# Attention masks copied ahead of the values' low part, and the buffers of two weights opened at the end of the ordered stretch

## The chip, the core and the metric

The kernel runs on one core of a Trainium2 chip. Its engines are the matrix engine (PE, with its weight loads shown as PEld), VectorE (DVE), ScalarE (ACT), GpSimd (POOL) and SyncE (SP, which issues the DMAs). The metric is the device time of one execution in microseconds; the median of several runs is compared.

## The reference

A gated linear attention (4 batches, 8 heads, 768 tokens, head size 48) feeds two feed-forward blocks over 3072 tokens of width 384. The weights come as 64-bit floats, which the kernel converts to 32 bits itself.

```python
for t in range(S):                                   # attention, f = sigmoid(f_logit)
    state = f[:, :, t, :, None] * state + np.einsum('bhd,bhe->bhde', k[:, :, t], v[:, :, t])
    y[:, :, t] = np.einsum('bhd,bhde->bhe', q[:, :, t], state)

h = x @ w_in                                         # first block, 384 -> 2048 -> 384
g = np.where(h > 0.0, h, np.exp(np.minimum(h, 0.0)) - 1.0)
x = g @ w_out

a = x @ w1; b = x @ w2                               # second block, 384 -> 1024 -> 1024 -> 384
out = (a * b @ w3) @ w_out2
```

## The kernel before

**Tiles and units.** The first block goes over 8 tiles of 384 tokens (j = 0 to 7), each in 16 units of 128 columns of the hidden layer (m = 0 to 15). Unit U = 16 j + m runs `p1_in(U)`: nine matmuls into a PSUM bank h (L640), two ACT passes (L643, L644) and one DVE pass (L646) that together make g, the ELU. From tile 1 on all operands are split into a high and a low part, so that three matmuls of reduced precision stand for one of full precision: `p1_split(U-1)` writes gh on ACT (L658) and then gl on DVE (L659), which needs gh. `p1_out(U-2)` multiplies both with w_out into three accumulators (nine matmuls, L672); at the end of a tile these are copied out (L679 on DVE, L681 on ACT) and stored.

**Attention.** While tile j runs, the attention of tile j+1 is computed in three chunks of 128 tokens, in steps that are spread over the units. For j > 0 the chunks begin at m = 0, 4 and 8, and their last steps fall on m = 6, 10 and 14: `b4` (scores on PE, L383, and a transposition of k, L389) comes one unit before; `b5` copies the scores through the causal mask into `amat`, two copies on DVE (L397), and k into kh on ACT (L399); `a4` multiplies values and old state (L444 on PE), then kh and values (L408) and evicts the result, which is the next tile's input (L453 on ACT, L455 on DVE). `b4`, `a4` and `a4k` take PSUM banks from a pool of three (`at`). The scans over the gates are L357 on DVE. The steps in `EARLY`, `b5` among them, are written ahead of `p1_in`, the others behind it. Within a unit the order of the code is `p1_split(U-1)`, early steps, `p1_in(U)`, late steps, `p1_out(U-2)`.

**Conversions.** Weights are loaded as pairs of words into staging tiles `wst` (`cv_load`, L492; four buffers) and converted in `rebias` (L226 on ACT with its readout), `rebiased_high` (L230, L231 on DVE) and `rebiased_low` (L236 on DVE). The jobs are numbered: 0 to 31 are w_in and w_out, 32 to 55 are w_out2 and w3, which `spill_step` splits and stores in DRAM one job in three units from unit 32 on (L554 on ACT, L560 on DVE, L562 the stores); 56 to 67 are w1 and w2, appended at m = 3, 7, 11 and 15 of tile 7 and split by `to_parts` (L538, L539). The results of jobs 32 to 67 go to `late["wt"]`, one tile of three parts in slot `wa7`, if the job's number modulo 4 is below 3, and otherwise to a buffer of its own called `wt`. `late["wt"]` is created at its first use, with job 32 in unit 32. In unit 108 `start_late` issues the loads of the stored w_out2 and w3 (o2 at L703, w3 at L713), whose product on PE (L725) follows the last units of the first block; then comes the second block (L883, L909).

**Order.** The units from 17 (`MAN`) up to 109 are traced under `manual_schedule`, in which an engine runs its instructions in the order of the code; `man.close()` ends this ahead of unit 110 (`MAN_B`). The rest is ordered by a planner. Every engine has its own in-order queue, and tiles are guarded by semaphores that the framework sets.

Of the kernel before, what the change touches and what calls it, by code (L numbers as in the profile page):

```python
# [9 lines left out]
F32 = mybir.dt.float32  # L10
F32R = mybir.dt.float32r
U32 = mybir.dt.uint32
# [28 lines left out]
CPT = TN // CH  # L41
NTILE = NT // TN
# [205 lines left out]
def main_path(ctx, tc, flag, qkf, vin, w_in, w_out, w1, w2, w3T, w_out2, ident_d, tri_d, x2_scr, o2_scr, w3_scr, out):  # L248
    nc = tc.nc
# [3 lines left out]
    wp = ctx.enter_context(tc.tile_pool(name="wp", bufs=1))  # L253
# [13 lines left out]
    keep = tri_f.bitcast(U32).unsqueeze(1).to_broadcast([128, NP, CH])  # L267
# [21 lines left out]
    def carve(name, dt, *cols):  # L289
        t = wp.tile([128, KD * 512], dt, name=name)  # L290
        o = np.cumsum((0,) + cols)
        return [t[:, int(a):int(b)] for a, b in zip(o, o[1:])]

    def by_pair(t):
        return t.rearrange("r (p t) -> r p t", p=NP)
# [4 lines left out]
    for c, (x, y) in enumerate((("wb4", "wb5"), ("wb6", "wb7")), 1):  # L300
        e, k = carve(x, F32, 512, 512)
# [4 lines left out]
    def buf(c, nm, make):  # L306
        return own[c][nm] if c < CPT and nm in own[c] else make()
# [16 lines left out]
    def a_load(c):  # L324
        if c < NCH:
            t = cx[c]["qkf"] = in_p.tile([PR, 3, NP, CH], F32, name="qkf")
            nc.sync.dma_start(out=t, in_=chunk(c))
            a_load_v(c)
# [14 lines left out]
    def khc(c):  # L343
        return buf(c, "kh", lambda: kh)

    def amats(c):
        return buf(c, "amat", lambda: amat)
# [43 lines left out]

    c_ps = {}

    def b5(c):
        ps = c_ps.pop(c)
        for e in range(2):
            nc.vector.copy_predicated(out=amats(c)[e], mask=keep, data=by_pair(ps[e]))  # L397
        if len(ps) > 2:
            nc.scalar.activation(out=khc(c).rearrange("t p r -> t (p r)"), in_=ps[2][:, 0:NP * PR], func=AF.Copy)  # L399

    def a4k(c):
        if c % CPB == CPB - 1:
            return
        v = cx[c]["v"]
        kp = bank(c, 4)
        for i in range(NP):
            for e, (r, cc) in enumerate(blocks):
                nc.tensor.matmul(kp[r, 2 * D * i:2 * D * (i + 1)][:, cc], lhsT=khc(c)[:, i, r],  # L408
                                 rhs=v[:, i, V_AT[e]:V_AT[e] + D], start=True, stop=True)
        c_kp[c] = kp  # L410
# [65 lines left out]
    late = {}  # L476
# [42 lines left out]
    def cv_step(k=1):  # L519

        while cv["split"] < cv["main"]:
            cv_split()
        i = cv["main"]
        k = min(k, len(jobs) - i)
        while cv["load"] < i + k:
            cv_load()
        while cv["abs"] < i + k:
            cv_abs()
        cv["main"] += k
        rebiased_to_f32(nc, [cvt[x] for x in range(i, i + k)])  # L530
        while cv["load"] < min(i + k + ST_BUFS - 2 + (3 if i < 2 * MF - 8 else 0), len(jobs)):
            cv_load()
        while cv["abs"] < min(cv["load"], i + k + (2 if i < 2 * MF else 1)):
            cv_abs()
# [7 lines left out]
    def spill_step(n, early):  # L542

        i, phase = cv["main"], n % 3
        if n == 0 and early:
            for _ in range(3):
                cv_load()
            cv_abs()
        st_, t = cvt[i]
        hi = st_.rearrange("p n two -> p (n two)")[:, 0:t.shape[1]].bitcast(F32)  # L550
        tf = t.bitcast(F32)
        if early:
            if phase == 2:
                nc.scalar.activation(out=hi.bitcast(F32R), in_=tf, func=AF.Copy)  # L554
        elif phase == 0:
            rebiased_high(nc, st_, t)
        elif phase == 1:
            rebiased_low(nc, st_, t)
        else:
            nc.vector.tensor_tensor(out=tf, in0=tf, in1=hi, op=ALU.subtract)  # L560
            for d, x in zip(jobs[i][2], (hi, tf)):
                nc.sync.dma_start(out=d, in_=x)  # L562
            cvt.pop(i)
            cv["main"] += 1
            cv["split"] += 1
            cv_load()
            cv_abs()
# [35 lines left out]
    def low(m, o):  # L603
        k = m // 4 * 2 + o
        while cv["split"] < at_job[o, m]:
            cv_split()
        nc.vector.tensor_tensor(out=stripe("l", k, m), in0=stripe("f", k, m), in1=stripe("h", k, m).bitcast(F32),
                                op=ALU.subtract)
# [3 lines left out]
    def job_12(q, a):  # L612
        if a == 0:
            w12[q] = [wp.tile([128, KD, 2, 256], F32R, name=slot(x, 2 * q)) for x in "hl"]
        srcs = []
        for e, w in enumerate((w1_u, w2_u)):
            srcs.append((lambda f, e=e: f[:, 512 * e:512 * e + 512],
                         w[128 * a:128 * a + 128, 512 * q:512 * q + 512]))
        jobs.append((512, srcs, to_parts(*[x[:, a].rearrange("p e n -> p (e n)") for x in w12[q]]), None))
# [29 lines left out]
    def p1_split(U):  # L649
        if U >= NU:  # L650
            return
        g = gs[U]
        if U < MF:
            gs[U] = (g,)
            return
        gh = g_p.tile([128, TN], F32R, name="gh")
        gl = g_p.tile([128, TN], F32R, name="gl")
        nc.scalar.activation(out=gh, in_=g, func=AF.Copy)  # L658
        nc.vector.tensor_tensor(out=gl, in0=g, in1=gh.bitcast(F32), op=ALU.subtract)  # L659
        gs[U] = (gh, gl)  # L660
# [24 lines left out]
    def start_spill():  # L685
        for k in range(M2):
            jobs.append((DM, [(whole(DM), wo2_u[128 * k:128 * k + 128, :])], [o2_scr[x, :, k] for x in range(2)], None))
        for i in range(M2):
            for k0 in (0, 4):
                src = w3T_u[128 * k0:128 * (k0 + 4), 256 * i:256 * (i + 1)].rearrange("(k p) n -> p k n", p=128)  # L690
                jobs.append((512, [(lambda f: f[:, 0:1024].rearrange("p (k n) -> p k n", k=4), src)],
                             [w3_scr[x, :, i, 128 * k0:128 * k0 + 512] for x in range(2)], None))
# [87 lines left out]
    def fill():  # L780
        if quota[0] < 0:
            spill_step(-1 - quota[0], False)
        elif quota[0] > 0:
            cv_step(quota[0])
        quota[0] = 0

    steps = (a_clamp, b0, b1, b2, b3, b4, b5, a4)
    psteps = steps[1:] + (a5,)
    wt = acc_p.tile([128, 512], F32, name="acc2")
# [14 lines left out]
    def slots(at, off):  # L804
        s = {}
        for i in range(CPT):
            for k in range(len(off)):
                s.setdefault(at[i] + off[k], []).append((i, k))
        return s

    at_slots = [slots(ATT_AT0, ATT_OFF0), slots(ATT_AT, ATT_OFF)]
    lows = [(4 * q + i, o) for q in range(MF // 4) for o in range(2) for i in range(4)]
    for U in range(NU + LAG):
        j, m = divmod(U, MF)
        if U == MAN:
            man.enter_context(tc.manual_schedule())
        if U == MAN_B:
            man.close()
        if j == 0:
            while cv["main"] < at_job[0, m]:  # L820
                cv_step()
            quota[0] = T0_JOBS
        while lows and 2 * MF - len(lows) < 2 * (U - MF) + 4:
            low(*lows.pop(0))
        if U == SPILL_AT:
            start_spill()
        if SPILL_AT <= U < SPILL_AT + 3 * 3 * M2:
            spill_step(U - SPILL_AT, True)
            quota[0] = SPILL_AT - U - 1
        elif U >= SPILL_AT and cv["split"] < len(jobs):  # L830
            quota[0] = 1
        if U >= 1:
            p1_split(U - 1)
        todo = at_slots[j > 0].get(m, []) if j < NTILE - 1 else []
        for early in (1, 0):
            for i, k in todo:
                if (k in EARLY) == early:
                    c = CPT * (j + 1) + i
                    steps[k](c)
                    if k == len(steps) - 1:  # L840
                        a_load(c + 2)
            if early and U < NU:
                p1_in(U, fill)
        if j == 0 and m >= LAG:
            while cv["main"] < at_job[1, m - LAG]:
                cv_step()
        p1_out(U - LAG)
        while quota[0] > 0:
            fill()
        if j == NTILE - 2 and m == LATE_AT:  # L850
            start_late()
        if j == NTILE - 1 and m % 4 == 3:
            for a in range(KD):
                job_12(m // 4, a)
        r = U - ((NTILE - 1) * MF + 3 + LAG)
        if 0 <= r < M2:
            if r:
                w3_load(r + 1)
            w_rows(r)
        if m == 10 and j == NTILE - 1:  # L860
            p2_load(0)
        if m == 14 and j == NTILE - 1:
            p2_split(0)
# [57 lines left out]
    for U in range(N2 + LAG):  # L921
        j, m = divmod(U, M2)
# [87 lines left out]
```

## Time and profile before

| | us |
|---|---|
| median of 3 runs | 869.1 (868.42 to 871.12) |
| profiled execution, its own time | 869.29 |
| its span in the profile | 867.4 |

| engine | busy us | share of the span |
|---|---|---|
| PE | 844.8 | 97% |
| PEld | 742.8 | 86% |
| DVE | 477.0 | 55% |
| ACT | 412.7 | 48% |
| POOL | 25.9 | 3% |

The chain of work that ended last lies on PE for 85% of the span, on DVE for 5%, on ACT for 4% and on DMAs for 3%. In a list in order of time a row has the start, the duration, the engine, the line and operation, what is written and read, and, in brackets, how long the engine was idle before it and what ended that. A row with a count above one is a run of equal instructions, and its duration that of all of them. Matmuls are pipelined, so the rows of PE overlap. In the table by stretches each engine has its busy time and number of instructions; PEclk is the clock granted to PE as a share of its upper level.

### The profile page before, as it was taken

Reading aid. Unit: us, or ns where it says so; the run is one execution under the profiler, and the core shown is the slowest. Engines: PE = TensorE matmul, PEld = TensorE weight load, DVE = VectorE, ACT = ScalarE, POOL = GpSimd, SP = SyncE. Lnnn points to the kernel's source line nnn. Section 1 sums busy time; section 2 is a strip of 40 time slices with the busy share of each in tenths; the row PEclk is TensorE's granted clock in tenths of the full one; section 3 lists DMA queues with packets and bytes.
Section 4 is the critical chain, followed back from the end, with each engine's and each line's share of the span. In section 5 each row is a group of like instructions: output and inputs, shape, how many; then the busy total and the mean of one; then the engine's idle time right before and its main releaser. Section 6 shows DMA issues by size and latency. Waiting matters only on the chain.

```text
span 867.4 us, 14383 instructions
## 1 busy us (share of the span) xinstructions
PE 844.8 (97%) x5768; PEld 742.8 (86%) x5768; DVE 477.0 (55%) x958; ACT 412.7 (48%) x863; POOL 25.9 (3%) x44
## 2 busy tenths in 40 slices
PE   7899999999999999999999999999999999999996
PEld 7566799989989999989889999988888888888885
DVE  7999388577577677677775552642323232222221
ACT  5886455566666665665664642531313222221211
POOL 3000000000000000001000000000000000000000
PEclk8999999999999999999999999999999999999999
DMA  9873211443444534445550765220201101000101
GB/s 274 261 239 114 67 47 44 134 116 112 145 128 141 168 115 129 157 139 177 167 164 22 305 199 172 85 64 1 73 1 37 37 0 37 1 36 1 37 1 40
DMA packets 47178, 90.79 MB, mean 105 GB/s; under 512 B 4144, under 2 KB 26928, under 8 KB 46848
## 3 DMA queue, kind: packets, MB, share of 16 engines
q1 hardware_dynamic: 47104, 89.80, 33.3%
q8 instruction: 47, 0.77, 0.4%
q14 instruction: 27, 0.22, 0.1%
HBM read 68.81 MB, written 20.97 MB: 104 GB/s over the span
## 4 chain that ended last, share of the span: by engine, by line
PE 85%; DVE 5%; ACT 4%; DMA 3%; issue 1%; SPq 0%; POOL 0%; ACTq 0%; DVEq 0%; POOLq 0%
PE acc L672 20%; PE h L640 19%; PE h L883 11%; PE at L883 11%; PE acc L909 11%; PE at L444 4%; PE at L725 4%; PE at L383 2%; PE at L408 1%; ACT gh L658 1%; PE at L389 1%; DMA qkf<-qkf_dram 1%; DMA wst<-moe_w_dram 1%; DMA wst<-moe_w_out_dram 1%; DVE g L646 1%
## 5 line engine op out<-in xcount | busy, mean ns | idle before, releaser
L672 PE MATMUL acc<-gh,wa 128*128 128x384 f32 x432 | 146.8, 370 | 0.0
L891 DVE TENSOR_TENSOR a<-at,a 128x512 f32<-128x512 f32 x48 | 33.2, 692 | 179.5 <-PE at L883 179.5
L640 PE MATMUL h<-xh,wa 128*128 128x384 f32 x348 | 117.9, 377 | 2.8 <-DVE gh L646 1.7
L672 PE MATMUL acc<-gh,wb 128*128 128x384 f32 x336 | 116.5, 348 | 2.1 <-ACT o L681 2.1
L640 PE MATMUL h<-xh,wb 128*128 128x384 f32 x336 | 113.2, 337 | 0.0
L672 PE MATMUL acc<-gl,wb 128*128 128x384 f32 x336 | 112.7, 336 | 0.0
L640 PE MATMUL h<-xl,wb 128*128 128x384 f32 x336 | 112.3, 334 | 0.0
L643 ACT ACTIVATE r<-h 128x384 f32<-128x384 f32 x128 | 62.0, 484 | 94.9 <-PE h L640 94.3
L646 DVE SCALAR_TENSOR_TENSOR g<-r,h 128x384 f32<-128x384 f32 x112 | 61.8, 552 | 74.8 <-ACT r L644 74.8
L672 PEld LDWEIGHTS acc<-gh,wa 128*128 128x128 f32 x432 | 80.9, 188 | 11.0 <-issue 0.2
L659 DVE TENSOR_TENSOR gl<-g,gh 128x384 fp32r<-128x384 f32 x112 | 62.6, 559 | 45.7 <-ACT gh L658 44.7
L658 ACT ACTIVATE gh<-g 128x384 fp32r<-128x384 f32 x112 | 58.6, 523 | 53.0 <-DVE g L646 52.2
L889 ACT ACTIVATE a<-h 128x512 f32<-128x512 f32 x48 | 28.7, 597 | 114.1 <-PE h L883 114.1
L640 PEld LDWEIGHTS h<-xh,wa 128*128 128x128 f32 x348 | 65.4, 188 | 15.8 <-DVE gh L646 2.3
L644 ACT ACTIVATE r<-r 128x384 f32<-128x384 f32 x128 | 67.1, 524 | 3.6
L672 PEld LDWEIGHTS acc<-gh,wb 128*128 128x128 f32 x336 | 63.2, 188 | 4.9 <-ACT o L681 2.7
L672 PEld LDWEIGHTS acc<-gl,wb 128*128 128x128 f32 x336 | 63.3, 189 | 0.1
L640 PEld LDWEIGHTS h<-xh,wb 128*128 128x128 f32 x336 | 63.1, 188 | 0.4
L640 PEld LDWEIGHTS h<-xl,wb 128*128 128x128 f32 x336 | 63.1, 188 | 0.4
L883 PE MATMUL h<-wb,wb 128*128 128x512 f32 x144 | 56.1, 390 | 0.0
L883 PE MATMUL h<-wa,wb 128*128 128x512 f32 x144 | 56.0, 389 | 0.0
L883 PE MATMUL at<-wa,wb 128*128 128x512 f32 x144 | 56.0, 389 | 0.0
(152 smaller groups left out, 1494.7 us busy)
## 6 DMA issues: line engine op xcount, KB each, us to landing
qkf<-qkf_dram SPq DMA_DIRECT2D x21, 672.0 KB, 5.8
wst<-moe_w_out_dram SPq DMA_DIRECT2D x24, 384.0 KB, 3.8
wst<-moe_w_dram SPq DMA_DIRECT2D x16, 512.0 KB, 4.2
wst<-moe_w_in_dram SPq DMA_DIRECT2D x16, 384.0 KB, 4.7
wst<-moe_w_dram SPq DMA_DIRECT2D x24, 256.0 KB, 3.8
v<-vin_dram SPq DMA_DIRECT2D x23, 224.0 KB, 5.7
out_dram<-wa SPq DMA_DIRECT2D x18, 256.0 KB, 2.1
w_scr<-wst SPq DMA_DIRECT2D x16, 256.0 KB, 2.1
```

The source lines that it names most:

```text
L444: nc.tensor.matmul(yp[32 * i:32 * i + 32, a * CH:(a + 1) * CH], lhsT=w[:, i, w0:w0 + 32], rhs=x[:, i, :], start=(n == 0), stop=(n == len(o ...
L640: nc.tensor.matmul(hp, lhsT=lw, rhs=rx, start=(n == 0), stop=(n == len(ops) - 1))
L643: nc.scalar.activation(out=r, in_=hp, func=AF.Relu, scale=-1.0)
L644: nc.scalar.activation(out=r, in_=r, func=AF.Exp, scale=-1.0)
L646: nc.vector.scalar_tensor_tensor(out=g, in0=r, scalar=-1.0, op0=ALU.add, in1=hp, op1=ALU.max)
L658: nc.scalar.activation(out=gh, in_=g, func=AF.Copy)
L659: nc.vector.tensor_tensor(out=gl, in0=g, in1=gh.bitcast(F32), op=ALU.subtract)
L672: nc.tensor.matmul(accs[j][i], lhsT=lw[:, 0, c], rhs=rg, start=(m == 0 and n == 0), stop=(m == MF - 1 and n == len(ops) - 1))
L725: nc.tensor.matmul(p, lhsT=lw[:, k, :], rhs=ro[:, k, :], start=(n == 0), stop=(n == 3 * M2 - 1))
L883: nc.tensor.matmul(p, lhsT=lw[:, a, e, c], rhs=rx[:, a, :], start=(n == 0), stop=(n == 3 * KD - 1))
L891: nc.vector.tensor_tensor(out=cc, in0=ps[1], in1=av, op=ALU.mult)
L909: nc.tensor.matmul(accs[j][i], lhsT=lw[:, m % 4, c], rhs=rc, start=(m == 0 and n == 0), stop=(m == M2 - 1 and n == 2))
```

## The change

In units whose early steps hold a `b5` and whose tile is above 0, the two mask copies are taken out of `b5` and issued ahead of `p1_split(U-1)`; the copy of kh stays in `b5`'s place. At unit 110, before the ordered stretch is closed, a new `late["wt"]` is created in slot `wa7`, and one column of each of its three parts is set to zero on DVE.

```diff
-    def b5(c):
+    def b5m(c):
+        for e in range(2):
+            nc.vector.copy_predicated(out=amats(c)[e], mask=keep, data=by_pair(c_ps[c][e]))
+
+    def b5k(c):
         ps = c_ps.pop(c)
-        for e in range(2):
-            nc.vector.copy_predicated(out=amats(c)[e], mask=keep, data=by_pair(ps[e]))
         if len(ps) > 2:
             nc.scalar.activation(out=khc(c).rearrange("t p r -> t (p r)"), in_=ps[2][:, 0:NP * PR], func=AF.Copy)
+
+    def b5(c):
+        b5m(c)
+        b5k(c)
...
         if U == MAN_B:
+            late["wt"] = wp.tile([128, 3 * 512], U32, name="wa7")
+            nc.vector.memset(late["wt"].bitcast(F32).rearrange("p (x n) -> p x n", x=3)[:, :, 0:1], 0.0)
             man.close()
...
+        todo = at_slots[j > 0].get(m, []) if j < NTILE - 1 else []
+        masks = [CPT * (j + 1) + i for i, k in todo if steps[k] is b5 and j > 0]
+        for c in masks:
+            b5m(c)
         if U >= 1:
             p1_split(U - 1)
-        todo = at_slots[j > 0].get(m, []) if j < NTILE - 1 else []
         for early in (1, 0):
             for i, k in todo:
                 if (k in EARLY) == early:
                     c = CPT * (j + 1) + i
-                    steps[k](c)
+                    (b5k if steps[k] is b5 and c in masks else steps[k])(c)
```

## Rows read from the trace of the kernel before

**Rows 1.** Busy time by stretch: 410 to 480 us.

```profile
core 0: us, PE busy (x) PEld busy (x) DVE busy (x) ACT busy (x) POOL busy (x), PEclk, DMA share, GB/s
...
410.00:480.00 70.00, 66.17 (x561) 62.41 (x560) 46.99 (x96) 39.69 (x84) 2.46 (x5) 0.98 0.43 133
```

**Rows 2.** Rows in order of time: unit m=6 of tile 3, ahead of the masks.

```profile
242.31 1.16 PE L383 MATMUL at<-qkf 48*128 48x128 f32 x16
...
245.54 0.56 DVE L646 SCALAR_TENSOR_TENSOR g<-r,h 128x384 f32<-128x384 f32 x1 [0.70 <-ACT r L644]
...
246.12 0.53 ACT L658 ACTIVATE gh<-g 128x384 fp32r<-128x384 f32 x1 [0.62 <-DVE g L646]
...
246.56 0.53 ACT L399 ACTIVATE kh<-at 128x448 f32<-128x448 f32 x1
...
246.68 0.56 DVE L659 TENSOR_TENSOR gl<-g,gh 128x384 fp32r<-128x384 f32 x1 [0.59 <-ACT gh L658]
...
247.16 1.33 DVE L397 COPY_PREDICATED amat<-tri_f,at 128x512 f32<-128x512 uint32 x2
```

**Rows 3.** PE in order of time: `a4` undisturbed (122, 202) and waiting (248, 310).

```profile
122.14 1.14 PE L444 MATMUL at<-amat,v 128*32 128x128 f32 x32
...
202.39 0.43 PE L444 MATMUL at<-qkf,state 112*32 112x128 f32 x8
...
204.07 0.56 PE L408 MATMUL at<-v,kh 128*48 128x48 f32 x16
...
247.98 1.43 PE L444 MATMUL at<-amat,v 128*32 128x128 f32 x32 [0.80 <-ACT r L643]
...
309.91 0.42 PE L444 MATMUL at<-qkf,state 112*32 112x128 f32 x8
...
312.27 0.56 PE L408 MATMUL at<-v,kh 128*48 128x48 f32 x16
```

**Rows 4.** PE in order of time: `a4` at m=14 of tiles 3, 4, 5, 6.

```profile
280.80 0.43 PE L444 MATMUL at<-qkf,state 112*32 112x128 f32 x8
...
343.32 0.42 PE L444 MATMUL at<-qkf,state 112*32 112x128 f32 x8
...
405.53 0.42 PE L444 MATMUL at<-qkf,state 112*32 112x128 f32 x8
...
473.46 0.43 PE L444 MATMUL at<-qkf,state 112*32 112x128 f32 x8
```

**Rows 5.** Users of `wst`, 400 to 480 us: count, durations (ns), first and last start.

```profile
L226 ACT ACTIVATE wa<-wst x5: 649/660/691, 406.6 to 435.7; 128x512 f32<-128x512 f32 x5
...
L226 ACT ACTIVATE wt<-wst x2: 656/666/676, 431.2 to 448.6; 128x512 f32<-128x512 f32 x2
...
L560 DVE TENSOR_TENSOR wa<-wa,wst x3: 676/685/689, 404.8 to 432.5; 128x512 f32<-128x512 f32 x3
...
L560 DVE TENSOR_TENSOR wt<-wt,wst x1: 993/993/993, 444.0 to 444.0; 128x512 f32<-128x512 f32 x1
```

**Rows 6.** Rows in order of time: tile 6, ACT, PE and DVE.

```profile
415.93 0.66 ACT L226 ACTIVATE wa<-wst 128x512 f32<-128x512 f32 x1 [2.58 <-DMA wst<-moe_w_dram]
416.49 0.19 ACT L226 ACTIVATION_READ_ACCUMULATOR wa<-wst 128x1 f32 x1
...
422.08 0.44 PE L672 MATMUL acc<-gh,wb 128*128 128x384 f32 x1 [1.60 <-ACT o L681]
...
437.34 0.68 DVE L231 SCALAR_TENSOR_TENSOR wa<-wst,wa 128x512 uint32<-128x512 uint32 x1
...
438.55 0.43 PE L444 MATMUL at<-qkf,state 112*32 112x128 f32 x8 [1.49 <-ACT kh L399]
```

**Rows 7.** Busy time by stretch, columns as in rows 1: 439 to 445 us.

```profile
439.00:445.00 6.00, 5.73 (x76) 5.02 (x77) 5.84 (x14) 2.80 (x6) 1.21 (x2) 0.72 0.53 127
```

**Rows 8.** Stretch 470 to 490 us; o2 and w3: issue, landing (us, 475 to 500), first use.

```profile
470.00:490.00 20.00, 20.00 (x163) 19.43 (x162) 8.29 (x15) 9.43 (x20) 0.00 (x0) 1.00 0.68 263
...
L703 SPq DMA_DIRECT2D o2h<-o_scr x1: 326/326/326, 475.4 to 475.4; - x1
...
w3l<-w_scr SPq DMA_DIRECT2D x2, 512.0 KB, 12.4
...
L725 PEld LDWEIGHTS at<-o2h,w3h x64: 187/188/188, 498.5 to 550.7; 128*128 128x128 f32 x64
```

## The prediction

> **What bounds the kernel now.** The page's first table has the matrix engine (PE) busy for 97% of the span, so a change can pay only where PE waits or where its clock is lowered. I read the table by stretches first: in 410 to 480 us PE is idle for 70.00 - 66.17 = 3.8 us at a mean clock of 0.98 [rows 1], and from 470 to 490 us it doesn't stop [rows 8]. Next I read PE's rows around the attention steps, which carry the reason of each wait, then DVE and ACT just ahead of those waits. Last I compared like with like: the time from one tile's last attention step to the next tile's [rows 4].
>
> Two things come out.
>
> First, **waits at the same place of five tiles**. In unit m=6 the step `a4` needs the two mask copies of `b5`, and in tiles j=2 to 6 PE is there before them. DVE ends g at 246.10, stands while ACT writes gh, then writes gl, and only then copies the masks, 247.16 to 248.49 [rows 2]. PE is idle for 0.80 us, and its mask matmuls then take 1.43 us instead of the undisturbed 1.14, since the second copy isn't there either [rows 3]. At the other thirteen sites (m=10, m=14, and m=6 of tile 1) the step runs without such a wait; 202.39 to 204.07 is one of them [rows 3].
>
> Second, **tile 6 is too long**. From L444 at m=14 to L444 at m=14 of the next tile it is 343.32 - 280.80 = 62.52 us for tile 4, and 473.46 - 405.53 = 67.93 us for tile 6, with the same work in the code [rows 4]. What differs is that conversions of w1 and w2 run there. The code appends these jobs in unit 115 and later, behind the ordered stretch. But between 400 and 480 us L226, a conversion's first pass, ran 5 + 2 = 7 times, where four jobs of w3 ended (L560, 3 + 1), the first of them begun before 400 us: three passes belong to w3, four to w1 and w2 [rows 5]. So the planner pulls instructions from behind the ordered stretch into it, as soon as buffers are free. There they do harm: ACT stands for 2.58 us in front of a load with a unit's ELU queued behind it, and PE then waits 1.60 us for an accumulator's copy; later a conversion's L231 stands between g and gl, ahead of the masks, and PE waits 1.49 us [rows 6]. Behind these waits the clock falls to a mean of 0.72 of its upper level of 2.4 GHz over 439 to 445 us [rows 7], which is PE partly at 1.2 GHz: (1 - 0.72) x 6.0 = 1.7 us of work lost.
>
> **The change part by part.**
>
> *Masks.* Nothing is added; the two copies of 18 attention steps move on DVE from behind gl to ahead of it. kh stays on ACT behind gh. The copies read the scores that PE's L383 wrote in the unit before, from 242.31 to 243.47, long before g ended at 246.10 [rows 2]. So the pair starts when g ends and runs beside gh: 246.10 to 246.10 + 1.33 = 247.43, the first copy done by about 246.80. PE's idle time began at 247.98 - 0.80 = 247.18. By then the first copy is there, and kh too (246.56 + 0.53 = 247.09); the second comes perhaps 0.1 us late. Gain: 0.80 + (1.43 - 1.14) - 0.1 = 1.0 us [rows 2, 3]. Tile 5 repeats it. In tiles 2 and 4 the step begins with matmuls on the old state, which need no mask and start when kh is written, before and after; only what follows gets shorter: 312.27 - 309.91 = 2.36 us, undisturbed 204.07 - 202.39 = 1.68, so 0.68 for each [rows 3]. Together 2 x 1.0 + 2 x 0.68 = 3.36 us for tiles 2 to 5.
>
> Behind the copies DVE now has gl, the scans, the fill jobs and the next g. gl starts up to 0.8 us later, and PE reads it in `p1_out` two units on, so the cover is more than a unit; the scans and all behind them come about 0.5 us *earlier*, since DVE no longer idles for gh (0.59 us at that gl) [rows 2]. Were the scores later than g somewhere, the copies would hold gl by what is missing, and that cover would take it.
>
> What PE waits for next at m=6 is the PSUM bank of `a4`. In tile 6 its first matmuls need no mask and yet wait 1.49 us until kh is copied [rows 6]: they wait for the bank that this copy frees. If the planner gives them the bank that the first mask copy frees, they could start at 246.80 instead of 247.09, 0.3 us better at each of five sites at most; with the bank of the second copy, at 247.43, 0.3 us worse. Between -1.5 and +1.5 us; I take 0, for kh's bank is the one with a row. The Trainium skill (Perfetto Trace Analysis, Optimization Strategy) warns that the same gap repeating on the engine that should be saturated can mean too little PSUM for the next tile. By it the gap would shift to the bank: that is the worse end, 1.5 us of the sum, and the 1.49 us row is such a wait; that of 0.80 us is not, for kh was written before it ended.
>
> *The buffers of w1 and w2.* Added are a new tile in slot `wa7` and a memset of three columns on DVE, as the last step of the ordered stretch. The memset has no row: between nothing and one mask copy of 512 columns, 0.67 us [rows 2]; for three columns 0.1, no gain in it, and DVE is free for 11.7 us of 470 to 490 [rows 8]. Its wait for the old tile is over by then, for the last w3 job in that slot (L560, 432.5) lies 35 us back [rows 5]. Its effect is a gate: it belongs to the ordered stretch and can't be pulled forward, and the jobs whose number modulo 4 is below 3 write into that tile, so three of the four early conversions come behind it. The fourth uses the other buffer and can stay where it is. Then tile 6 should run as tile 4 does: 67.93 - 62.52 = 5.41 us less, and the masks give it tile 4's 0.68 [rows 3, 4]. Sum 6.09. The waits shown (1.60, 1.49, and 1.7 for the clock) make 4.8 of the 5.41. Bounds: nothing, if the gate doesn't hold, to 6.1.
>
> Where they go: a conversion is one ACT pass of 0.66 us and its readout of 0.19, and three DVE passes of at most 0.69 [rows 5, 6]; three of them are 2.6 us of ACT and at most 6.2 of DVE, in 470 to 490 us, where these have 10.6 and 11.7 us free [rows 8]. Their DMAs move too: staging buffers come free later, so up to three jobs' loads (0.5 MB each) land beside those of o2 and w3, which SP issues from 475.4 on. Those are 5 MB, the last one issued by 478 and landed 12.4 us later, at about 490.5; PE wants them at 498.5 [rows 8]. Another 1.5 MB at 5 MB in 15 us are 4.5 us: 495, still ahead of 498.5. Cost 0, and the cover is 3.5 us.
>
> *The clock.* It was at its upper level over 470 to 490 us and fell behind a run of waits [rows 6 to 8]. I take it that it stays up when these are gone; if not, 1.7 us stay.
>
> *Sum.* The profiled execution itself took 869.29 (span 867.4 and 1.9 around it): 869.29 - 3.36 - 6.09 = 859.84. The median of the runs shown is 0.2 lower, so 859.7.
>
> **The rivals.**
> *Masks only* (the gate doesn't hold, or the planner pulls other work in): 3.36 + 0.68 = 4.0 us, so 865.1. For it: whether the gate reaches the planner, no row shows. Against: four conversions came early and every one with a free buffer, so a free buffer is what let them in.
> *Better, not well*: the clock still falls, the bank is the late one, or the bunched conversions delay a unit. 1.5 to 3.5 us stay: 861.2 to 863.2.
> *Slower.* The place is SP's queue. The loads of o2 and w3 go out at 475.4 and are wanted 23 us later. If the planner puts job loads ahead of them in this queue, loads which wait for staging buffers that only the gated conversions free, they go out when those conversions are done. The 3.5 us of cover go first; behind that each microsecond costs one. With 9.4 us gained before, the kernel is slower by over 0.3% from 3.5 + 9.4 + 2.6 = 15.5 us of delay on: 872 or more. For it: the queue is in order, and gated conversions are work of low rank. Against: ACT and DVE are half free there [rows 8], and the conversions need 6 us.
> *No effect*: neither part reaches PE, 869.
>
> **How the numbers follow.** Forecast 859.7: 0.62; better, not well: 0.15; masks only: 0.13; no effect: 0.05; slower: 0.05. The range goes down to 857.5 (the bank's better end and some spread between runs) and up past masks only, 865.6. About 0.3%, or 2.6 us, is what a measurement can tell from no change; of masks only a little falls inside it. Faster 0.87, same 0.08, slower 0.05.
>
> **What would show it.** DVE's mask copies start right behind g, ahead of gl; no wait on L397 at m=6 of tiles 2 to 6; before the memset only one w1 or w2 conversion; tile 6 takes some 61.8 us, without the 1.60 us wait and with a clock of 1.00 over 410 to 480 us; PE never idle from there to L725. Wrong it is if conversions still run in units 97 to 103, if PE waits at m=6 for a bank as long as it did for masks, or if the first L725 waits for a DMA.

## The result, and the profile of the changed kernel

The changed kernel takes 860.65 us (median; 859.75 to 862.24) beside 870.0 for the kernel before in the same runs: a ratio of 0.9896, 95% interval 0.987 to 0.9921, so 9.0 us or 1.0% faster. Measured once more, beside the experiments below, it took 859.79 against 869.22, a ratio of 0.9888 (0.9871 to 0.9904). The profiled execution took 861.49 with a span of 859.6.

The unit that the masks were moved in, m=6 of tile 3, in order of time (start, duration, engine, line; in brackets the idle time ahead and what ended it). Most line numbers of the changed kernel are six higher; the masks are L396, kh L401, `a4` L450, g L652, gh L664, gl L665.

```profile
246.20 0.56 DVE L652 SCALAR_TENSOR_TENSOR g<-r,h 128x384 f32<-128x384 f32 x1 [0.70 <-ACT r L650]
246.67 1.37 DVE L396 COPY_PREDICATED amat<-tri_f,at 128x512 f32<-128x512 uint32 x2
246.79 0.53 ACT L664 ACTIVATE gh<-g 128x384 fp32r<-128x384 f32 x1 [0.62 <-DVE g L652]
247.22 0.53 ACT L401 ACTIVATE kh<-at 128x448 f32<-128x448 f32 x1
247.77 1.19 PE L450 MATMUL at<-amat,v 128*32 128x128 f32 x32
247.92 0.56 DVE L665 TENSOR_TENSOR gl<-g,gh 128x384 fp32r<-128x384 f32 x1
```

The masks start with g's end and run beside gh. The idle time ahead of PE's step is gone, and its matmuls take 1.19 us where they took 1.43 [rows 2, 3].

The step `a4` at m=14 of tiles 3 to 6, the same four places as in rows 4:

```profile
280.31 0.42 PE L450 MATMUL at<-qkf,state 112*32 112x128 f32 x8
...
342.06 0.43 PE L450 MATMUL at<-qkf,state 112*32 112x128 f32 x8
...
403.15 0.43 PE L450 MATMUL at<-qkf,state 112*32 112x128 f32 x8
...
465.59 0.43 PE L450 MATMUL at<-qkf,state 112*32 112x128 f32 x8
```

Tile 6 now takes 465.59 - 403.15 = 62.44 us, where it took 67.93; tile 4 takes 61.75, where it took 62.52 [rows 4]. The same place in tiles 1 and 2 is at 154.61 and 218.56 us in the kernel before, and at 156.00 and 219.23 in the changed one. So tiles 2 to 6 got shorter by 0.72, 1.16, 0.77, 1.12 and 5.49 us, together 9.26. The profiled times differ by 869.29 - 861.49 = 7.8 only, because this execution came 1.4 us later through its start, which the change doesn't touch in the code: it was behind by as much at the last `a4` of tile 0 (93.17 us against 91.72). Behind m=14 of tile 6 both need the same time to the end, 393.9 and 394.0 us of span.

By stretches: span of the stretch, then PE, its weight loads, DVE, ACT and POOL with instruction counts, the granted clock, the DMA share and GB/s. The first two are stretches of rows 1 and 7. The last two are the same place of the code in both kernels, 20 us that begin 2.69 us ahead of `a4` at m=14 of tile 6: at 462.90 us in the changed kernel, at 470.77 in the kernel before.

```profile
core 0: us, PE busy (x) PEld busy (x) DVE busy (x) ACT busy (x) POOL busy (x), PEclk, DMA share, GB/s
410.00:480.00 70.00, 69.44 (x592) 66.80 (x591) 48.56 (x101) 43.35 (x91) 2.42 (x4) 1.00 0.42 139
439.00:445.00 6.00, 6.00 (x45) 5.75 (x45) 3.19 (x7) 1.88 (x5) 0.00 (x0) 1.00 0.43 154
...
462.90:482.90 20.00, 20.00 (x162) 19.55 (x162) 12.76 (x26) 11.48 (x25) 0.00 (x0) 1.00 0.70 263
...
470.77:490.77 20.00, 20.00 (x162) 19.55 (x162) 8.30 (x16) 9.38 (x19) 0.00 (x0) 1.00 0.72 278
```

PE's idle time in 410 to 480 us went from 3.8 to 0.56 us and its clock stays at the upper level of 2.4 GHz [rows 1, 7]. The work that was held back shows in the last two lines, the changed kernel's first: ACT has 2.1 us more than before, DVE 4.5 more, and PE is busy throughout in both. The stretch from 470 to 490 us [rows 8] can't be compared directly, for there the changed kernel is some 8 us further in its work.

The gate and what it holds, in order of time; the job loads and those of o2 in SP's queue, with what the last two job loads waited for; and w3's landing and the first use of o2 and w3 (us):

```profile
444.74 0.67 ACT L226 ACTIVATE wt<-wst 128x512 f32<-128x512 f32 x1 [2.55 <-DMA wst<-moe_w_dram]
...
449.42 0.43 PE L450 MATMUL at<-qkf,state 112*32 112x128 f32 x8 [0.39 <-DVE amat L396]
...
462.87 0.06 DVE L825 MEMSET wa<- 128x3 f32 x1
...
463.38 0.66 ACT L226 ACTIVATE wa<-wst 128x512 f32<-128x512 f32 x1
...
464.03 0.67 ACT L226 ACTIVATE wa<-wst 128x512 f32<-128x512 f32 x1
...
464.68 0.68 ACT L226 ACTIVATE wa<-wst 128x512 f32<-128x512 f32 x1
...
467.19 0.80 SPq L498 DMA_DIRECT2D wst<-moe_w_dram  x2
468.40 0.33 SPq L709 DMA_DIRECT2D o2h<-o_scr  x1
...
SPq L498 <- DVE wa L236: 18.4, 1, 18.4
...
w3l<-w_scr SPq DMA_DIRECT2D x2, 512.0 KB, 13.8
...
L731 PEld LDWEIGHTS at<-o2h,w3h x64: 187/188/188, 490.6 to 542.8; 128*128 128x128 f32 x64
```

Three conversions start behind the memset. The fourth, in buffer `wt`, stays inside the ordered stretch, and ACT stands 2.55 us in front of its load. PE has 0.39 us of waiting a little later. In SP's queue two job loads (467.19) stand ahead of o2's (468.40); they waited 18.4 us, until a gated conversion's last pass (L236) had freed a staging buffer. o2's load goes out 2.81 us behind `a4` at m=14 of tile 6; in the kernel before it is 1.93 us (475.39 against 473.46).

### The profile page after: what moved, and what is told of

Same layout as the page of the kernel before. It is cut to its first block, busy times and chain, and to the rows that moved or that the text cites. A ratio compares the mean times of both kernels' runs of the same rounds, so it can differ in the third digit from the quotient of the medians.

```text
span 859.6 us, 14361 instructions
## 1 busy us (share of the span) xinstructions
PE 841.7 (98%) x5768; PEld 742.5 (86%) x5768; DVE 475.9 (55%) x959; ACT 413.3 (48%) x863; POOL 25.6 (3%) x44
## 4 chain that ended last, share of the span: by engine, by line
PE 89%; DVE 3%; ACT 3%; DMA 3%; issue 1%; SPq 0%; ACTq 0%; DVEq 0%
PE acc L678 21%; PE h L646 20%; PE h L894 11%; PE at L894 11%; PE acc L920 11%; PE at L450 4%; PE at L731 4%; PE at L383 3%; PE at L414 1%; PE at L389 1%; DMA qkf<-qkf_dram 1%; DMA wst<-moe_w_out_dram 1%; ACT gh L664 1%; DVE g L652 1%; DMA w_scr<-wst 1%
## 5 line engine op out<-in xcount | busy, mean ns | idle before, releaser
L652 DVE SCALAR_TENSOR_TENSOR g<-r,h 128x384 f32<-128x384 f32 x112 | 61.7, 551 | 73.6 <-ACT r L650 73.4
L665 DVE TENSOR_TENSOR gl<-g,gh 128x384 fp32r<-128x384 f32 x112 | 62.2, 556 | 39.5 <-ACT gh L664 39.1
L664 ACT ACTIVATE gh<-g 128x384 fp32r<-128x384 f32 x112 | 58.5, 523 | 52.8 <-DVE g L652 51.3
```

The costliest lines, as they stand in the source:

```text
L652: nc.vector.scalar_tensor_tensor(out=g, in0=r, scalar=-1.0, op0=ALU.add, in1=hp, op1=ALU.max)
```

## The experiments

All medians stand beside runs of the kernel before on the same chip, 869.1 to 869.3 us. Tile 6 is from `a4` at m=14 of tile 5 to the same place of tile 6, as in rows 4.

| kernel | median, us | ratio (95%) | tile 6, us |
|---|---|---|---|
| before, three profiles | 869.1 to 869.3 | 1 | 67.93, 66.84, 67.69 |
| masks alone, two profiles | 863.24 | 0.9943 (0.9926 to 0.9959) | 64.70, 65.22 |
| gate alone | 866.51 | 0.9976 (0.9964 to 0.9989) | 64.47 |
| gate for all four, no masks | 865.67 | 0.9963 (0.9951 to 0.9975) | 63.01 |
| masks at m=6 only, gate | 861.51 | 0.9925 (0.9908 to 0.9942) | 63.66 |
| the change, two profiles | 859.79 | 0.9888 (0.9871 to 0.9904) | 62.44, 62.45 |
| masks, gate for all four | 859.63 | 0.99 (0.9883 to 0.9916) | 61.98 |
| the same, tile 2's loads early | 860.04 | 0.9888 (0.987 to 0.9905) | 61.99 |
| the change, gate some 16 us later | 861.33 | 0.9909 (0.9888 to 0.9931) | 62.59 |

### The masks alone

The change without its last hunk:

```diff
-            late["wt"] = wp.tile([128, 3 * 512], U32, name="wa7")
-            nc.vector.memset(late["wt"].bitcast(F32).rearrange("p (x n) -> p x n", x=3)[:, :, 0:1], 0.0)
             man.close()
```

> Masks moved as in the changed kernel, no new tile and no memset at the end of the ordered stretch. Theory (two separate gains, one of the masks at m=6 of tiles 2 to 6, one of the gate in tile 6): tiles 2 to 5 as short as in the changed kernel (together 3.8 us shorter than before), tile 6 still long, 66.5 to 67.5 us from L444 at m=14 to L444 at m=14, because four w1 and w2 conversions still run in it; about 865.6 us against 870.0 before. Rival (the masks carry nearly the whole gain, and tile 6 was long only because the masks came late): 861 to 862, tile 6 near 62.5 us.

Measured: 863.24 us, and tile 6 at 64.70 us, well under the 66.5 to 67.5 expected. Tiles 3 to 5 were as in the changed kernel (61.06, 61.75, 61.07); tile 2 took 62.36 us, 0.9 less than in the changed kernel with the same code. DVE, ACT and PE at m=6 of tile 6:

```profile
432.84 0.43 DVE L230 TENSOR_SCALAR wa<-wa 128x512 uint32<-128x512 uint32 x1 [1.09 <-ACT wa L226]
433.25 0.55 DVE L652 SCALAR_TENSOR_TENSOR g<-r,h 128x384 f32<-128x384 f32 x1
433.72 1.34 DVE L396 COPY_PREDICATED amat<-tri_f,at 128x512 f32<-128x512 uint32 x2
...
434.27 0.52 ACT L401 ACTIVATE kh<-at 128x448 f32<-128x448 f32 x1
...
434.59 0.43 PE L450 MATMUL at<-qkf,state 112*32 112x128 f32 x8 [1.64 <-DVE amat L396]
```

The early conversions are all still there and PE still waits 1.64 us behind one of them. What went with the masks alone is the fall of the clock (it is 1.00 in every stretch of tile 6) and part of the wait for the accumulator's copy, 0.70 us instead of 1.60 (1.30 in a second profile, below). The prediction had counted the clock to the gate.

A second thing is to be seen here: PE's first matmuls at 434.59 need no mask and start while kh is still being copied (434.27 to 434.79). By the row's releaser and these times they wait for the bank that the *first mask copy* frees, at about 434.4, and not for kh's.

### The gate alone

The last hunk of the change alone, masks where they were.

> New tile and memset at the end of the ordered stretch, masks where they were before. Theory: no w1 or w2 conversion but one before the memset, tile 6 near 62.5 us instead of 67.9, clock 1.00 over the whole of tile 6, and the waits for masks at m=6 as before in tiles 2 to 6; about 864.6 us. Rival (the gate is of no use without the masks): 868 or more, PE still idle for over 1 us at m=6 of tile 6. A second rival, on the clock: if one of the remaining mask waits alone lowers it, it falls below 1.00 at m=6 of tile 6 here too.

Measured: 866.51 us and tile 6 at 64.47 us, 2 us longer than expected. The three conversions are gone from it, and the clock is 1.00; but PE waits 0.50 + 0.29 us at m=6 and again at m=10. ACT, PE and DVE at m=10 of tile 6:

```profile
449.26 0.67 ACT L226 ACTIVATE wt<-wst 128x512 f32<-128x512 f32 x1 [2.55 <-DMA wst<-moe_w_dram]
...
449.93 0.51 ACT L658 ACTIVATE gh<-g 128x384 fp32r<-128x384 f32 x1
...
453.61 0.53 ACT L399 ACTIVATE kh<-at 128x448 f32<-128x448 f32 x1
...
454.28 0.42 PE L444 MATMUL at<-qkf,state 112*32 112x128 f32 x8 [0.74 <-ACT kh L399]
...
454.98 0.42 PE L444 MATMUL at<-amat,v 128*32 128x128 f32 x8 [0.28 <-DVE amat L397]
```

This is the fourth conversion, which the gate leaves where it is: ACT stands 2.55 us in front of its load, gh and then kh come late, and PE pays 0.74 + 0.28 us. In the changed kernel the same stand costs 0.39 us, since the masks no longer stand behind gl.

### The gate for all four buffers, with the masks and without

The fourth buffer is allocated and written at the same place, and the job takes it from there:

```diff
+            late["w4"] = cv_p.tile([128, 512], U32, name="wt")
+            nc.vector.memset(late["w4"].bitcast(F32)[:, 0:1], 0.0)
             man.close()
...
```

> The changed kernel, and the fourth early conversion (job 59, the buffer called wt) is held back by a memset of its own at the same place. Theory (an early conversion costs by standing on ACT in front of its load: 2.55 us in the changed kernel, and PE then waits 0.39 us for masks at m=10 of tile 6): that wait goes, tile 6 takes 61.8 instead of 62.4 us, 860.1 us in all. Rival (the stand on ACT is covered, and four bunched conversions cost something in tile 7 instead): 860.7 or up to 2 us more.

> The gate for all four buffers, masks where they were. With the gate of three alone tile 6 took 64.47 us, with waits of 0.50 + 0.29 us at m=6 and 0.74 + 0.28 at m=10 on kh and the masks. Theory (the parts overlap: at m=10 ACT is late by its stand in front of the fourth conversion's load, and the masks' move gives DVE the time to make up for that): without the fourth conversion the m=10 waits go, 1.02 us, tile 6 takes 63.4; only 0.8 to 1.0 us of masks stay at m=6. Median 865.4. Rival (the waits at m=10 come with the order of DVE's work alone): tile 6 stays at 64.4 or more, median 866.5.

Measured with the masks: 859.63 us, tile 6 at 61.98 us and no wait at m=10; that is 0.46 us less in tile 6 than the change has, as expected, and too little to tell in the median (859.79 for the change). The change had been measured again for this: 860.2 to 861.0 was expected if the fourth conversion costs its 0.5 us, 859.6 if it costs nothing, and 859.79 decides neither. Without the masks: 865.67 us, tile 6 at 63.01 us. There ACT goes straight from gh to kh, and PE's step comes without a wait:

```profile
450.26 0.52 ACT L661 ACTIVATE gh<-g 128x384 fp32r<-128x384 f32 x1 [0.62 <-DVE g L649]
450.69 0.53 ACT L399 ACTIVATE kh<-at 128x448 f32<-128x448 f32 x1
...
453.02 0.43 PE L444 MATMUL at<-qkf,state 112*32 112x128 f32 x8
```

So the m=10 waits of the gate alone do come from the fourth conversion, and by the length of tile 6 it costs 64.47 - 63.01 = 1.46 us there. What is left to the masks in tile 6, once no conversion is in it, is 63.01 - 61.98 = 1.03 us, that of a tile with a wait at m=6 (tiles 3 and 5: 62.28 to 61.07, 62.20 to 61.06).

### The masks moved at m=6 only

```diff
-        masks = [CPT * (j + 1) + i for i, k in todo if steps[k] is b5 and j > 0]
+        masks = [CPT * (j + 1) + i for i, k in todo if steps[k] is b5 and j > 0 and i == 0]
```

> The changed kernel with the masks moved at m=6 only; at m=10 and m=14 they stand behind gl as before. Theory (only at m=6 does PE get to the masks first; elsewhere they were hidden): within 0.5 us of the changed kernel, 860.7, save perhaps at m=10 of tile 6 where ACT is late. Rival (the 0.5 us of VectorE time saved at each of the other twelve steps counts too): up to 3 us slower, 862 to 864.

Measured: 861.51 us. Tiles 3 to 5 are as in the change (61.16, 61.74, 61.06): there the moves at m=10 and m=14 are worth nothing, as the prediction had it. In tile 6 they are worth 1.2 us, for behind the fourth conversion's stand PE waits for kh and the masks again:

```profile
448.42 0.56 DVE L665 TENSOR_TENSOR gl<-g,gh 128x384 fp32r<-128x384 f32 x1 [0.59 <-ACT gh L664]
...
448.89 1.34 DVE L396 COPY_PREDICATED amat<-tri_f,at 128x512 f32<-128x512 uint32 x2
...
448.96 0.42 PE L450 MATMUL at<-qkf,state 112*32 112x128 f32 x8 [0.94 <-ACT kh L401]
...
449.67 0.43 PE L450 MATMUL at<-amat,v 128*32 128x128 f32 x8 [0.28 <-DVE amat L396]
```

Here kh is copied ahead of the masks, and the bank is kh's again. At every place where PE's matmuls on the old state had to wait, the releaser named is the copy that ran first. The order in the code is not what decides: `b5` has the masks ahead of kh in the kernel before too. How the bank is chosen isn't shown.

### Is the fall of the clock there each time?

The kernel before and the masks alone, profiled again without a change.

> The kernel before, once more, with a profile: are tile 6's losses the same each time? Theory (all of it follows from the order of work, which is fixed): tile 6 takes 67.5 to 68.3 us again, with the waits of 1.6 and 1.5 us, and the granted clock over 439 to 445 us falls to 0.7 to 0.75 behind them. Rival (the clock's fall was chance in one execution): tile 6 takes 66.0 to 66.5 us, with the same waits and a clock of 1.00. Either way about 869.

> The kernel before, a third profile, beside the masks alone: theory (the waits in tile 6 bring the fall each time, at one place or the other): the clock falls for some 3 us within tile 6, which takes 66.5 to 68 us. Rival (chance): no fall, tile 6 takes 65 to 66 us with the waits still there.

> The masks alone, once more: is the fall of the clock gone with them, or did it stay out by chance? The kernel before showed it in both of its executions, at 440 to 443 us in one and at 424.4 to 427.6 in the other, each time 3 us at half speed behind a run of waits; the masks alone still have waits of 0.7 and 1.6 us there, without a fall. Theory (fewer waits, no fall): tile 6 takes 64.2 to 65.0 us again at a clock of 1.00. Rival (chance): a fall of some 1.7 us in tile 6, 65.8 to 66.5 us.

The kernel before, second profile: PE's two waits, and the stretches around the first. A granted clock of 1.00 is the upper level, 2.4 GHz; 0.50 is the lower, 1.2 GHz.

```profile
422.87 0.44 PE L672 MATMUL acc<-gh,wb 128*128 128x384 f32 x1 [1.84 <-ACT o L681]
...
422.00:424.00 2.00, 1.13 (x6) 1.13 (x7) 1.21 (x3) 2.00 (x6) 0.00 (x0) 1.00 0.95 299
424.00:426.00 2.00, 2.00 (x10) 2.00 (x9) 2.00 (x7) 1.29 (x3) 0.00 (x0) 0.60 0.99 354
426.00:428.00 2.00, 2.00 (x8) 2.00 (x7) 2.00 (x5) 0.76 (x2) 0.00 (x0) 0.55 0.51 162
...
439.07 0.43 PE L444 MATMUL at<-qkf,state 112*32 112x128 f32 x8 [0.19 <-ACT kh L399]
```

Its third profile:

```profile
422.14 0.44 PE L672 MATMUL acc<-gh,wb 128*128 128x384 f32 x1 [1.79 <-ACT o L681]
...
438.32 0.43 PE L444 MATMUL at<-qkf,state 112*32 112x128 f32 x8 [1.46 <-ACT kh L399]
...
438.00:440.00 2.00, 1.40 (x28) 1.09 (x32) 2.00 (x5) 1.08 (x3) 0.00 (x0) 0.76 0.00 0
440.00:442.00 2.00, 2.00 (x42) 1.52 (x36) 1.88 (x5) 0.12 (x1) 0.00 (x0) 0.50 0.04 6
442.00:444.00 2.00, 2.00 (x24) 1.93 (x21) 1.53 (x4) 2.00 (x5) 0.62 (x2) 0.88 0.94 267
```

And the masks alone, second profile:

```profile
418.62 0.44 PE L678 MATMUL acc<-gh,wb 128*128 128x384 f32 x1 [1.30 <-ACT o L687]
...
434.88 0.43 PE L450 MATMUL at<-qkf,state 112*32 112x128 f32 x8 [1.54 <-DVE amat L396]
...
434.00:436.00 2.00, 1.12 (x41) 1.15 (x45) 2.00 (x5) 1.83 (x4) 0.00 (x0) 1.00 0.00 0
436.00:438.00 2.00, 2.00 (x45) 1.75 (x37) 2.00 (x6) 0.82 (x3) 0.00 (x0) 1.00 0.40 86
```

The kernel before lost the same amount in each profile: (0.40 + 0.45) x 2 = 1.7 us here, (0.24 + 0.50 + 0.12) x 2 = 1.7 there, 1.7 in the first [rows 7]. But it lost it behind different waits: once behind the first, of 1.84 us, twice behind the second, of 1.46 and 1.49. Where it fell early, PE came later to the second wait, which shrank from 1.49 to 0.19 us, and tile 6 took 66.84 us and not 67.9. So the expectation for the second profile missed with both its numbers: the fall was neither where it had been nor gone. The masks alone, with waits of 0.70 + 1.64 and 1.30 + 1.54 us, had no fall in either profile, so its absence there is no single chance; but 1.30 and 1.54 are close to 1.79 and 1.46, and what decides between them isn't settled by these runs. The Trainium skill (TensorE: Matmul & The Clock Gate, A second HAM failure mode: psum-queue depth-cycling) says that short idle times of TensorE between groups of matmuls, as it goes through its PSUM banks, can make the clock go back and forth between its two levels. The rows of the kernel before agree in so far as the clock fell behind such waits, once in each profile and at a cost of 1.7 us; those of the masks alone show waits of nearly the same length that didn't bring it.

### The gate later still

This tries the rival by which the kernel would have become slower. The memset becomes a copy from unit 113's gl:

```diff
-            nc.vector.memset(late["wt"].bitcast(F32).rearrange("p (x n) -> p x n", x=3)[:, :, 0:1], 0.0)
...
+        if U == MAN_B + 4:
+            nc.vector.tensor_copy(out=late["wt"].bitcast(F32).rearrange("p (x n) -> p x n", x=3)[:, :, 0],
+                                  in_=gs[U - 1][1].bitcast(F32)[:, 0:3])
```

> The changed kernel with the memset replaced by a copy from unit 113's gl, so that the three buffers open some 14 us later, at about 477 us instead of 462.9. This tries the rival that ends slower: the place is SP's queue, where o2 and w3 are loaded at 468.4 us and wanted at 490.8. Theory (the loads of o2 go out ahead of what the gate holds back, and the conversions have slack): they still go out by 470 us, PE doesn't stop between 470 and 500 us, the median stays within 0.5 us of 859.8. Rival (job loads that wait for staging buffers stand ahead of them in the queue): they go out at 482 or later, land some 12 us behind that, PE waits 3 us or more at its first product with o2, and the median is 863 or more.

```profile
466.26 0.33 SPq L709 DMA_DIRECT2D o2h<-o_scr  x1
...
479.21 0.66 ACT L226 ACTIVATE wa<-wst 128x512 f32<-128x512 f32 x1
...
470.00:490.00 20.00, 20.00 (x117) 20.00 (x116) 13.98 (x28) 14.44 (x34) 0.00 (x0) 1.00 0.90 338
```

The first gated conversion starts at 479.21 us, some 16 us later, and the load of o2 still goes out at 466.26, ahead of the job loads, which follow at 482.56. The trace shows no wait of PE from 455 us on. But this run doesn't try what it was meant to try. In the changed kernel job loads do stand ahead of o2's in SP's queue (467.19 and 468.40, in the section on the result); with the later gate the planner puts o2's first, 1.93 us behind `a4` at m=14 of tile 6 as in the kernel before. What a gate 16 us later would cost with the job loads in front is not shown. The median is 861.33 us, 1.5 over the change and outside the 0.5 expected; the two intervals overlap (0.9888 to 0.9931 and 0.9871 to 0.9904), the change's own first runs go from 859.75 to 862.24, the profiled execution's span (858.5 us) is no longer than the change's (859.2 to 859.6), and the trace has no wait for it. Whether the later gate costs something stays open.

### Tile 2's loads earlier

In the profile with all four buffers gated, tile 2 is longer than its neighbours, 63.25 us; in the other profiles with the masks moved, where its code is the same, it takes from 62.36 to 63.23 us. The first three loads of the weights that it spills were issued four units earlier:

```diff
-            for _ in range(3):
-                cv_load()
...
-        if U == SPILL_AT:
+        if U == SPILL_AT - 4:
             start_spill()
+            for _ in range(3):
+                cv_load()
```

> All four buffers gated, masks ahead, and the first three loads of the weights that tile 2 spills issued four units earlier. With all four gated, tile 2 alone is still longer than its neighbours: 63.25 us against 61.1 to 61.75, with ACT standing 2.62 us in front of that load and PE 0.77 us in front of an accumulator's copy behind it. Theory (an in-order ACT in front of a transfer is the rest of the loss): the load is there when ACT comes, the 0.77 us wait goes, tile 2 takes 62.3 to 62.5, the median falls by 0.8 to 1.0 us, to 858.7 or so. Rival (the stand is where it is because ACT runs ahead of its work, and tile 2 is longer by its own work): tile 2 stays above 63 us and the median within 0.3 us of 859.6.

The trace does what was expected and a little more: ACT's stand of 2.62 us and PE's wait of 0.77 us are gone, and tile 2 takes 61.74 us, 1.5 less than there and 0.6 less than the shortest of the others. The median doesn't show it: 860.04 us (857.73 to 861.74) beside 859.79 for the change and 859.63 without this edit. Executions of this kernel differ by 4 us among themselves, and the way to `a4` at m=6 of tile 1, through the start, takes from 122.1 to 124.8 us over the profiles of all these kernels (124.72 in this one). A gain of 1 us can't be told from none here, and no version is shown to beat the change.

## Why the prediction was right, and where its steps were off

The forecast was 859.7 us and the time 860.65 and 859.79. The sum of 9.45 us (3.36 for the masks in tiles 2 to 5, 6.09 for tile 6) stands against 9.26 us in the tiles of the two profiles shown, and 8.7 by the means of the three profiles before and the two after. Some of the agreement is luck: the profile that the sum was read from had the longest tile 6 of the three. Its steps:

**Masks in tiles 2 to 5: held.** 3.36 us forecast, 0.72 + 1.16 + 0.77 + 1.12 = 3.77 measured. The order is the one described: masks from g's end on, gl behind them, `p1_out` two units on not held up. Tiles 3 and 5 gave 0.1 to 0.2 us more each than the 1.0 worked out. The 0.72 of tile 2 is uncertain by some 0.9 us, the spread of this tile between profiles with the same code.

**The PSUM bank: the value held, the reason didn't.** The prediction took nothing, "for kh's bank is the one with a row". In the runs the bank was that of the copy that ran first: kh's before, the first mask copy's after. That was the better end of the range given, and at m=6 of tile 6 it is worth some 0.2 us (in the masks alone PE starts at 434.59, where kh's copy ended at 434.79). PE's wait for a bank that is left at m=6 came to 0.23 us in tile 2 and 0.16 in tile 6; tiles 3 to 5 have none. The Trainium skill (Perfetto Trace Analysis, Optimization Strategy) says that a gap that repeats on the engine that should be saturated can mean too little PSUM for the next tile. Here the gap of 0.80 us that repeated went when DVE's work was put in another order, and only the 0.16 and 0.23 us can be of that kind.

**Tile 6: the sum held roughly, its split between the parts didn't.** 6.09 us was forecast, 0.68 for the masks and 5.41 for the gate. The profiles give 5.49, and 4.4 to 5.5 with the other profiles of the kernel before. Taken singly against its mean of 67.5 us, the masks alone give 2.5 us (65.0) and the gate alone 3.0 (64.47). With all four conversions held back and no masks moved it is 63.01, so 4.5 us for the conversions and the clock, and the masks add 1.03. Three terms were mis-sized:
- The *clock's fall*, 1.7 us, was counted to the gate. Either part alone is without it. In the gain of the change it counts once, but it belongs to the gain of each part when that part is taken alone.
- The *masks in tile 6* were taken at tile 4's 0.68 us. They give 1.03 once no conversion is left in that tile.
- The *fourth conversion* "can stay where it is". By the length of tile 6 it costs 0.46 us in the change (62.44 against 61.98), 1.7 with the masks at m=10 behind gl (63.66 against the same 61.98), and 1.46 with no masks moved (64.47 against 63.01). The step that failed was to count three conversions as if all of the loss were theirs: it is enough that one is left whose load isn't there when ACT, which works in order, comes to it.

This is also why "masks only" was priced at 865.1 and measured 863.24, while the gate alone, expected at 864.6, measured 866.51. In tile 6 each part also takes away waits that the other leaves: the masks ahead of gl cut what the fourth conversion costs from 1.46 to 0.46 us, and the gate takes away the conversion behind which PE waits 1.64 us with the masks alone.

**Where the gated work goes: cost nothing, as forecast.** Over 20 us from the same place of the code on, ACT's added busy time is 11.48 - 9.38 = 2.1 us (2.6 worked out) and DVE's 12.76 - 8.30 = 4.5 (6.2 at most). The memset took 0.06 us (0.1 taken). The cover got thinner: w3's low parts landed 13.8 us behind their issue instead of 12.4 [rows 8], and from o2's issue to PE's first use it is 490.6 - 468.4 = 22.2 us, 23.1 before. These 0.9 us are what the two job loads in front of it took.

**The rivals.** *Masks only*, as "the gate doesn't hold", fell with the three conversions behind the memset. *Better, not well* was near: 0.55 us of waits at m=6 and m=10 of tile 6 were left, not 1.5. *Slower*, through SP's queue, had its premise right and its size wrong: job loads that wait for a gated conversion do stand ahead of o2's load, but the conversions were done early enough that this took 0.9 us, less than the 3.5 us of cover, and PE didn't wait. A longer hold with this order wasn't run. *No effect* was off by 9 us.

## What to carry to other kernels

When a planner may pull later work into a stretch whose order was tuned by hand, look at what it pulled in, and for each piece at what it waits for: one conversion in front of a load that hasn't landed makes an in-order engine late for everything behind it. Holding back a buffer by a write at the stretch's end is a cheap gate (0.06 us), but it has to cover every buffer through which the work can enter, and what stands in a DMA queue behind the held loads has to be looked at too. And before the waits of a region are shared out between two remedies, look whether each of them alone would take away the same one; a repeated profile of the kernel before shows which of its losses are the same each time.

## What was not expected of the hardware

The clock fell for some 3 us in each of three profiles of the same kernel, at one of two places 15 us apart, and cost 1.7 us each time: the amount was stable, the place wasn't. Behind waits of 1.30 and 1.54 us in the kernel with the masks alone it didn't fall. And the way to `a4` at m=6 of tile 1 took from 122.1 to 124.8 us over these profiles, which is as much as several of the edits are worth; single profiles were therefore compared tile by tile. The three of the kernel before (122.14, 122.80 and 122.45 us) are the shortest of all thirteen. So it is at the last `a4` of tile 0, ahead of which no edit touches the code. Whether this is chance stays open; the medians, 9.0 and 9.4 us apart, give no sign of a loss there.
